# Halved inverse steps in every quarter, more adding transfers, and a shared first rounding copy, in a kernel of an FNet layer beside an S4D convolution

## The chip, the cores and the metric

One core of a Trainium2 chip. Times are device microseconds of one launch; the kernel before took 569.42 us (median of three runs, 568.53 to 570.57). TensorE's granted clock was 0.998 of full speed.

## The reference

Two independent layers over 2048 positions and 512 channels of float32, laid side by side in the output:

```python
def _A_ref(x, dft_seq_re, dft_seq_im, dft_hid_re, dft_hid_im):
    a = jnp.einsum("bsd,ed->bse", x, dft_hid_re)
    b = jnp.einsum("bsd,ed->bse", x, dft_hid_im)
    return jnp.einsum("ts,bse->bte", dft_seq_re, a) - jnp.einsum("ts,bse->bte", dft_seq_im, b)

def _B_ref(u, log_A_real, A_imag, C_real, C_imag, log_dt, D_skip):
    dt = jnp.exp(log_dt)
    A = -jnp.exp(log_A_real) + 1j * A_imag
    C = (C_real + 1j * C_imag) * dt[:, None]
    P = jnp.exp((A * dt[:, None])[:, :, None] * pos[None, None, :])
    K = 2.0 * jnp.einsum("dn,dnl->dl", C, P).real
    y = irfft(rfft(u_t, 2L) * rfft(K, 2L))[:, :, :L]
    return y.transpose(0, 2, 1) + u * D_skip
```

## The kernel before

**Two streams on one TensorE.** FNet (class Fnet) is dense matmul work: x is multiplied by the sequence matrices S (8 groups of 16 tiles, "s" groups) and the results, parked in DRAM as `p`, by the hidden matrices (4 groups of 8 tiles, "p" groups). For precision each float32 tile is split into a rounded part hi and a remainder lo, and each product is three matmuls (hh, lh, hl) of 128x128 by 128x512: 1920 matmuls (L312), issued three at a time in 640 steps. The SSM (class Ssm) builds exponential tables on VectorE, forms the kernel K by small matmuls (L735), and convolves by two-stage Fourier transforms with small tiled matmuls (L779, L840, L975, L1009, L1133, L1098), interleaved with FNet's steps.

**How a moving tile is split.** A plain tile is loaded by SP into `raw` (L266), rounded into hi by ScalarE (L150) and subtracted into lo by VectorE (L155): `split`. A soft tile, one of `SOFTS`, is loaded by GpSimd's queue straight into hi with the rounding done by the transfer (L248); ScalarE writes -hi into lo (L251), and a second GpSimd transfer adds the source to lo (L253). There are five hi/lo pairs (DEPTH) and five raw buffers (RAWS). SOFTS holds 5 of the 16 tiles of each of the groups 1 to 7, 35 in all. The first S tile is loaded by ScalarE's queue, and TensorE's first product waits for it.

**The inverse steps.** Channels go in four quarters h of 128. After the second-stage products, `first_inverses` (L1009) writes a partial inverse through `zs` in DRAM; the last stage loads it again as `zl`. Quarters 0 and 1 use `inverse`: 16 matmuls with 128 rows of contraction and 64 columns for each of two blocks (L1133; the profile counts each float32 matmul twice, so x32). Quarters 2 and 3 (HALVED) use `inverse2`: VectorE first forms sum and difference of the two halves (L1089, L1091), then 32 matmuls (x64) with half the rows and 32 columns, eight side by side in the array (L1098). Quarter 2's two blocks run as one pair, quarter 3's as (3,0) and (3,1). Both kinds write 512 KB of output (L1145, L1119). Their constants are `ib`, and `ib2`, which is loaded over ib's place once the four old blocks are done (`load_ib2`).

**The order** of all instructions is written out by hand: `ORDER` lists, entry by entry, which generator goes one step further, and `TURNS` who takes PSUM banks next. Each engine and queue runs its share in that order. FNet's matmul generator is number 31 in the old list (640 entries of three matmuls) and 30 in the new. In the old tail 491 is product (3,3) with its first inverse (its fifth entry), 477 the pair of quarter 2, 494 and 505 the blocks (3,0) and (3,1); in the new one these are 496, 481, 497 and 505. An inverse's entries are its four load issues, its VectorE passes, its matmul block and its evictions. y tiles d0 to d3 of the last FNet group are evicted by ScalarE (L326, L321) and stored (L335, L322).

Of the kernel before, what the change touches and what calls it, by code (L numbers as in the profile page):

```python
# [26 lines left out]
def fft_constants():  # L27
# [24 lines left out]
    return [np.ascontiguousarray(a.astype(np.float32)) for a in (f1u, f1k, w2, ia, ib, ib2)]  # L52
# [70 lines left out]
class Fnet:  # L123
# [23 lines left out]
    def split(self, *tiles, n=None):  # L147
        yield "act"
        hi, _, src = tiles if n is None or n > 1 else self.first[self.turns["hi"].pop(0)]
        self.nc.scalar.activation(hi, src, AF.Copy)  # L150
        if not self.hi_ev.done:
            self.plan.set(self.hi_ev)
        yield "dve"
        hi, lo, src = tiles if n is None or n > 1 else self.first[self.turns["lo"].pop(0)]
        self.nc.vector.tensor_tensor(lo, src, hi.bitcast(F32), op=OP.subtract)  # L155
# [102 lines left out]
    def load(self, src, to, where, key, ev):  # L258
# [11 lines left out]
        yield from self.split(*to, raw)  # L270
# [76 lines left out]
class Ssm:  # L347


    def __init__(self, tc, ctx, plan, fnet, nd, ldt, dsk, uG, f1u, f1k, w2, ia, ib, ib2, out):  # L350
        self.tc, self.nc, self.plan, self.fnet = tc, tc.nc, plan, fnet
        self.nd, self.ldt, self.uG, self.ib2_in, self.out = nd, ldt, uG, ib2, out
# [8 lines left out]
        second, third = (("w2", w2), ("ib", ib)), (("ia", ia),)  # L361
# [8 lines left out]
        self.sets, self.set_ev, self.ib_ev, self.ib_left = {}, [Event(), Event()], Event(), 4  # L370
# [501 lines left out]
    def quarters(self):  # L872
# [11 lines left out]
        self.ib2_ev, self.loaded_ev = Event(), Event()  # L884
        self.pair, self.last, self.k_ev = [[] for _ in range(4)], [], Event()
        self.plan.spawn(self.load_ib2())
# [51 lines left out]
    def product(self, b, h, q, got, done):  # L938
# [65 lines left out]
        def run(got, o=0):  # L1004
            for c in range(2):
                for g in range(2):
                    for xx in range(4):
                        rows = slice(32 * xx, 32 * xx + 32)
                        nc.tensor.matmul(got[xx // 2][1][64 * g:64 * g + 64, xx % 2, o:o + 2 * PART], self.ia[rows, q // 2 if h >= HALVED else 0, c],  # L1009
                                         Y[c][rows, :, g], start=c == 0, stop=c == 1, tile_position=(32 * xx, 64 * g))  # L1010
# [42 lines left out]
    def inverses(self, h):  # L1053

        yield self.zs_ev[h][0]
        if h < 3:
            yield self.zs_ev[h][1]
        if h >= HALVED:
            yield self.set_ev[1]
        b = self.sets[int(h >= min(HALVED, 3))]  # L1060
        for i in range(2):
            yield b.zls
            self.plan.spawn((self.inverse2 if h >= HALVED else self.inverse)(b, h, i, 16))

    def load_ib2(self):
        yield self.ib_ev
        self.ib2 = self.ib[:, :16].rearrange("p n (a s) -> p n a s", a=2)
        yield "dma"
        self.nc.sync.dma_start(self.ib2, self.ib2_in)
        self.plan.set(self.ib2_ev)  # L1070

    def inverse2(self, b, h, i, n):
# [6 lines left out]
        for a in range(2):  # L1079
            yield self.zs_ev[h][a]  # L1080
            yield "act"
            nc.scalar.dma_start(z[64:, a], view[:, a, n * i + c:n * i + n])
            yield "dma"
            nc.sync.dma_start(z[:64, a], view[:, a, n * i:n * i + c])
        t = b.pool.tile([128, c, PART], F32, name="zsum", bufs=2 * b.n - 1)
        for w in range(0, c, 4):
            m = slice(w, w + 4)
            yield "dve"
            nc.vector.tensor_tensor(t[:, m], z[:, 0, m], z[:, 1, m], op=OP.add)  # L1089
            yield "dve"  # L1090
            nc.vector.tensor_tensor(z[:, 1, m], z[:, 0, m], z[:, 1, m], op=OP.subtract)  # L1091
# [13 lines left out]
        yield self.ib2_ev  # L1105
        got = yield from self.banks(len(two))
        yield "pe"
        for (_, _, run), (_, ps) in zip(two, got):
            run(ps)
        for (i, z, _), (k, ps) in zip(two, got):  # L1110
# [11 lines left out]
    def inverse(self, b, h, i, n):  # L1122

        nc = self.nc
        z = b.pool.tile([128, n, PART], F32, name="zl", bufs=b.n)
        yield "dma"
        for o in range(0, n, 8):
            nc.sync.dma_start(z[:, o:o + 8], self.zs[h].rearrange("s c l d -> (s c) l d")[:, n * i + o:n * i + o + 8])
        (k, ps), = yield from self.banks(1)
        yield "pe"  # L1130
        for w in range(n // 2):
            for y in range(2):
                nc.tensor.matmul(ps[64 * y:64 * y + 64, w // 4, PART * (w % 4):PART * (w % 4) + PART],  # L1133
                                 self.ib[:, n * i + 2 * w + y], z[:, 2 * w + y], start=True, stop=True,
                                 tile_position=(0, 64 * y))
        self.ib_left -= 1
        if not self.ib_left:
            self.plan.set(self.ib_ev)
        o = n * i // 2
        for w in range(0, n // 2, 4):  # L1140
            yield "act"
            nc.scalar.activation(z[:, w:w + 4], ps[:, w // 4].rearrange("p (w d) -> p w d", w=4), AF.Copy)
        self.give(k)
        yield "dma"
        nc.sync.dma_start(self.out[:, o:o + n // 2, PART * h:PART * h + PART], z[:, :n // 2])  # L1145
        self.plan.put(b.zls)


ORDER = [
# [185 lines left out]
```

## Time and profile before

| what | value |
|---|---|
| three runs, median | 569.42 us |
| profiled execution | 569.5 us, its span 567.7 us |
| TensorE busy | 559.3 us (99%), 6278 matmuls |
| VectorE busy | 505.6 us (89%) |
| ScalarE busy | 369.5 us (65%) |
| GpSimd busy | 50.3 us (9%) |
| DMA | 135.5 MB, 239 GB/s mean |
| chain that ended last, by line | L312 79%, L735 5%, L975 5%, L1009 3%, L840 2%, L779 1%, L1133 1%, L1098 1% |

How to read it: the span runs from the first to the last instruction of the profiled execution; the 1.8 us between it and the execution's time lie around it. PE is TensorE's matmuls, DVE VectorE, ACT ScalarE, POOL GpSimd, SP the queue that issues most DMAs; a q after an engine's name is its sequencer or DMA issue. "Lnnn" is a line of the kernel. The chain follows back, from the last instruction, what released each step. A wait's "issue" means that nothing the profile shows was waited for.

### The profile page before, as it was taken

How to read it: one execution, taken by the hardware profiler on the slowest of the kernel's cores; microseconds unless marked ns; L12 is line 12 of the kernel's file. 1: busy time of each engine (PE TensorE's matmuls, PEld its weight loads, DVE VectorE, ACT ScalarE, POOL GpSimd, SP SyncE). 2: the span in 40 equal slices, each digit the busy share in tenths (PEclk: the TensorE clock that was granted, in tenths of full speed). 3: DMA queues.
4: the chain of work that ended last, by engine and by line, in shares of the span. 5: the costliest groups of instructions: out<-in, count | busy, mean ns of one | idle time of the engine just before them, and what ended most of it. 6: DMA issues, size and time to landing. Idle time of an engine off the chain costs nothing.

```text
span 567.7 us, 15512 instructions
## 1 busy us (share of the span) xinstructions
PE 559.3 (99%) x6278; PEld 433.0 (76%) x6278; DVE 505.6 (89%) x846; ACT 369.5 (65%) x734; POOL 50.3 (9%) x74
## 2 busy tenths in 40 slices
PE   8999999999999999999999999999999999999995
PEld 6877776777878777777778778778787777777784
DVE  6979999999999999999999999999999998366640
ACT  5788736756686586868677776867876554355512
POOL 0001210021121112011111111111110000000000
PEclk9999999999999999999999999999999999999999
DMA  8989989998869858978799599679997899989776
GB/s 287 310 277 362 243 250 255 316 242 221 188 179 221 233 137 229 254 160 216 208 266 257 150 241 255 177 197 230 287 275 208 266 261 294 265 257 244 210 218 204
DMA packets 148855, 135.53 MB, mean 239 GB/s; under 512 B 47280, under 2 KB 107312, under 8 KB 148528
## 3 DMA queue, kind: packets, MB, share of 16 engines
q1 hardware_dynamic: 137776, 113.70, 67.2%
q0 software_dynamic: 10080, 18.35, 16.3%
q10 hardware_dynamic: 928, 2.49, 1.7%
q8 instruction: 49, 0.80, 0.6%
q14 instruction: 22, 0.18, 0.1%
HBM read 91.79 MB, written 42.73 MB: 237 GB/s over the span
## 4 chain that ended last, share of the span: by engine, by line
PE 98%; DMA 1%; ACT 0%; issue 0%
PE acc L312 79%; PE f L735 5%; PE f L975 5%; PE f L1009 3%; PE f L840 2%; PE f L779 1%; PE f L1133 1%; PE f L1098 1%; DMA raw<-in_sT 1%; ACT hi L150 0%; ACT y L321 0%; ACT zl L1113 0%
## 5 line engine op out<-in xcount | busy, mean ns | idle before, releaser
L312 PE MATMUL acc<-hi,x 128*128 128x512 f32 x1280 | 344.0, 395 | 0.3 <-ACT hi L150 0.3
L312 PEld LDWEIGHTS acc<-hi,x 128*128 128x128 f32 x1280 | 236.3, 188 | 67.5 <-issue 16.3
L312 PE MATMUL acc<-lo,x 128*128 128x512 f32 x640 | 189.6, 391 | 0.3 <-issue 0.3
L312 PEld LDWEIGHTS acc<-lo,x 128*128 128x128 f32 x640 | 119.7, 188 | 28.8 <-issue 3.3
L150 ACT ACTIVATE hi<-raw 128x512 fp32r<-128x512 f32 x125 | 77.2, 627 | 39.8 <-PE acc L312 19.3
L155 DVE TENSOR_TENSOR lo<-raw,hi 128x512 fp32r<-128x512 f32 x125 | 84.7, 686 | 20.0 <-ACT hi L150 15.6
L531 DVE TENSOR_TENSOR prod<-t,cs 128x128 f32<-128x128 f32 (+4 forms) x128 | 87.2, 695 | 1.1 <-ACT t L678 0.5
L547 ACT ACTIVATE square<-t 128x256 f32<-128x256 f32 (+1 forms) x64 | 36.8, 576 | 30.1 <-DVE t L540 25.8
L540 DVE TENSOR_TENSOR t<-prod 128x64 f32<-128x64 f32 (+4 forms) x128 | 53.0, 426 | 0.9
L253 POOL DMA_DIRECT2D lo<-in_sT x35 | 30.5, 872 | 246.6 <-ACT lo L251 134.0
L642 DVE TENSOR_TENSOR t<-t,cs 128x1024 f32<-128x1024 f32 x32 | 39.0, 1222 | 0.3
L648 DVE TENSOR_TENSOR t<-t,prod 128x1024 f32<-128x1024 f32 x32 | 39.1, 1221 | 0.1
L642 DVE TENSOR_TENSOR prod<-t,cs 128x1024 f32<-128x1024 f32 x32 | 39.0, 1220 | 0.0
L947 ACT ACTIVATE uk<-f 128x1024 f32<-128x1024 f32 x32 | 31.3, 1020 | 10.2 <-PE f L975 10.1
L326 ACT ACTIVATE y<-acc 128x512 f32<-128x512 f32 x47 | 26.7, 597 | 13.0 <-PE acc L312 13.0
L735 PEld LDWEIGHTS f<-t,t 128*32 128x32 f32 x2048 | 29.3, 110 | 5.5 <-issue 4.1
L248 POOL DMA_DIRECT2D hi<-in_sT x35 | 21.9, 626 | 127.2 <-PE acc L312 105.9
L735 PE MATMUL f<-t,t 128*32 128x64 f32 x2048 | 31.9, 220 | 0.0
L1037 ACT ACTIVATE z<-f 128x512 f32<-128x512 f32 x32 | 17.5, 603 | 19.8 <-PE f L1009 12.4
L251 ACT ACTIVATE lo<-hi 128x512 fp32r<-128x512 f32 x35 | 21.8, 624 | 10.6 <-DMA hi<-in_sT 10.3
L962 DVE TENSOR_TENSOR z<-uk 128x1024 f32<-128x1024 f32 (+1 forms) x20 | 20.1, 1009 | 7.4 <-ACT uk L947 7.3
L560 DVE TENSOR_TENSOR t<-square 128x128 f32<-128x128 f32 (+1 forms) x64 | 24.8, 388 | 1.1 <-ACT square L547 1.1
(107 smaller groups left out, 509.0 us busy)
## 6 DMA issues: line engine op xcount, KB each, us to landing
raw<-in_sT SPq DMA_DIRECT2D x92, 256.0 KB, 5.2
hi<-in_sT POOLq DMA_DIRECT2D x35, 256.0 KB, 5.7
lo<-in_sT POOLq DMA_DIRECT2D x35, 256.0 KB, 5.7
p<-y SPq DMA_DIRECT2D x32, 256.0 KB, 4.8
xk<-xk_sb SPq DMA_DIRECT2D x32, 256.0 KB, 4.7
zs<-z SPq DMA_DIRECT2D x32, 256.0 KB, 3.6
raw<-p SPq DMA_DIRECT2D x32, 256.0 KB, 5.1
xt<-xu SPq DMA_DIRECT2D x24, 256.0 KB, 5.1
```

The lines of the kernel that those rows point to most:

```text
L150: self.nc.scalar.activation(hi, src, AF.Copy)
L155: self.nc.vector.tensor_tensor(lo, src, hi.bitcast(F32), op=OP.subtract)
L253: self.nc.gpsimd.dma_start(lo, src, accum_op=OP.add)
L312: self.nc.tensor.matmul(acc[d], still["hl".index(p[0])][:, 128 * d:128 * d + 128], m["hl".index(p[1])], start=i is items[0] and p == "hh", ...
L531: self.nc.vector.tensor_tensor(p.rearrange("p k d c m -> p k (d c) m"), src.rearrange("p d c l -> p (d c) l")[:, None, :, rows].to_broadca ...
L540: self.nc.vector.tensor_tensor(dst[:, :, :, rows], p[:, 0], p[:, 1, :, ::-1], op=OP.add)
L547: self.nc.scalar.activation(sq, t[:, :, :, m // 2:m], AF.Square)
L642: self.nc.vector.tensor_tensor(dst, t[:, :, :, rows], seed[:, k, :, :, None].to_broadcast([128, CHUNK, 2, n // 2 // CHUNK]), op=OP.mult)
L648: self.nc.vector.tensor_tensor(dst, dst, p[:, :, ::-1], op=OP.add)
L735: nc.tensor.matmul(ps[32 * j:32 * j + 32, i], t1[:, d, c], t2[:, d, c], start=c == 0, stop=c == 1, tile_position=(0, 32 * j))
L947: a.activation(uk[:, r].rearrange("p g c n d -> p g (c n d)"), p, AF.Copy)
L975: nc.tensor.matmul(got[r][1][32 * xx:32 * xx + 32, g, 256 * c:256 * c + 256], self.w2[rows, 2 * q + r, xx, 32 * c:32 * c + 32], xt[rows].r ...
```

## The change

`inverse` and `load_ib2` go; the old `inverse2`, renamed `inverse`, serves all four quarters, with whole instead of halved VectorE passes, and for quarters 0 and 1 with its sum in a buffer of the z pool, which has three buffers in the first set instead of two. Only `ib2` is kept as a constant, and the output is unpacked on the host in one form. SOFTS holds 8 of 16 tiles of each group instead of 5, 56 in all. `split` takes a column `half`: for the first S tile ScalarE rounds columns 0 to 255 and VectorE columns 256 to 511. ORDER and TURNS are new throughout. The hunks that only rename or drop `ib` and the greater part of the order are left out.

```diff
-    def split(self, *tiles, n=None):
+    def split(self, *tiles, n=None, half=None):
         yield "act"
         hi, _, src = tiles if n is None or n > 1 else self.first[self.turns["hi"].pop(0)]
-        self.nc.scalar.activation(hi, src, AF.Copy)
+        self.nc.scalar.activation(hi[:, :half], src[:, :half], AF.Copy)
+        if half:
+            self.nc.vector.tensor_copy(hi[:, half:], src[:, half:])
...
-        yield from self.split(*to, raw)
+        yield from self.split(*to, raw, half=256 if key == self.items[self.groups[0]][0] else None)
...
-        second, third = (("w2", w2), ("ib", ib)), (("ia", ia),)
+        second, third = (("w2", w2), ("ib2", ib2)), (("ia", ia),)
...
-        self.plan.spawn(self.load_ib2())
...
-                        nc.tensor.matmul(got[xx // 2][1][64 * g:64 * g + 64, xx % 2, o:o + 2 * PART], self.ia[rows, q // 2 if h >= HALVED else 0, c],
+                        nc.tensor.matmul(got[xx // 2][1][64 * g:64 * g + 64, xx % 2, o:o + 2 * PART], self.ia[rows, q // 2, c],
...
-        yield self.zs_ev[h][0]
-        if h < 3:
-            yield self.zs_ev[h][1]
-        if h >= HALVED:
+        for a in range(1 + (h < 3)):
+            yield self.zs_ev[h][a]
+        if h > 1:
             yield self.set_ev[1]
-        b = self.sets[int(h >= min(HALVED, 3))]
+        b = self.sets[int(h > 1)]
         for i in range(2):
             yield b.zls
-            self.plan.spawn((self.inverse2 if h >= HALVED else self.inverse)(b, h, i, 16))
-
-    def load_ib2(self):
-        yield self.ib_ev
-        self.ib2 = self.ib[:, :16].rearrange("p n (a s) -> p n a s", a=2)
-        yield "dma"
-        self.nc.sync.dma_start(self.ib2, self.ib2_in)
-        self.plan.set(self.ib2_ev)
-
-    def inverse2(self, b, h, i, n):
+            self.plan.spawn(self.inverse(b, h, i, 16))
+
+    def inverse(self, b, h, i, n):
 
         nc, c = self.nc, n // 2
         z = b.pool.tile([128, 2, c, PART], F32, name="zl", bufs=2 * b.n - 1)
         view = self.zs[h].rearrange("(a s) c l d -> (s c) a l d", a=2)
         if h == 2:
             yield self.loaded_ev
-        for a in range(2):
-            yield self.zs_ev[h][a]
-            yield "act"
-            nc.scalar.dma_start(z[64:, a], view[:, a, n * i + c:n * i + n])
+        if h < 2:
             yield "dma"
-            nc.sync.dma_start(z[:64, a], view[:, a, n * i:n * i + c])
-        t = b.pool.tile([128, c, PART], F32, name="zsum", bufs=2 * b.n - 1)
-        for w in range(0, c, 4):
-            m = slice(w, w + 4)
-            yield "dve"
-            nc.vector.tensor_tensor(t[:, m], z[:, 0, m], z[:, 1, m], op=OP.add)
-            yield "dve"
-            nc.vector.tensor_tensor(z[:, 1, m], z[:, 0, m], z[:, 1, m], op=OP.subtract)
+            for y in range(2):
+                nc.sync.dma_start(z[64 * y:64 * y + 64], view[:, :, n * i + c * y:n * i + c * y + c])
+            yield b.zbs
+            t = b.pool.tile([128, c, PART], F32, name="z", bufs=b.zn)
+        else:
+            for a in range(2):
+                yield self.zs_ev[h][a]
+                yield "act"
+                nc.scalar.dma_start(z[64:, a], view[:, a, n * i + c:n * i + n])
+                yield "dma"
+                nc.sync.dma_start(z[:64, a], view[:, a, n * i:n * i + c])
+            t = b.pool.tile([128, c, PART], F32, name="zsum", bufs=2 * b.n - 1)
+        yield "dve"
+        nc.vector.tensor_tensor(t, z[:, 0], z[:, 1], op=OP.add)
+        yield "dve"
+        nc.vector.tensor_tensor(z[:, 1], z[:, 0], z[:, 1], op=OP.subtract)
...
-        yield self.ib2_ev
         got = yield from self.banks(len(two))
         yield "pe"
         for (_, _, run), (_, ps) in zip(two, got):
             run(ps)
+        if h < 2:
+            self.plan.put(b.zbs)
         for (i, z, _), (k, ps) in zip(two, got):
             for y in range(2):
...
-    def inverse(self, b, h, i, n):
...
 ORDER = [
...
-    485, 31, 485, 481, 31, 493, 492, 486, 31, 492, 31, 493, 31, 493, 468, 31, 491, 482, 31, 491, 31, 483, 478, 31,
-    477, 471, 31, 477, 489, 491, 494, 477, 494, 481, 478, 31, 478, 491, 487, 31, 495, 478, 491, 477, 31, 496, 491, 31,
-    491, 498, 31, 483, 497, 477, 499, 500, 482, 489, 482, 31, 477, 489, 31, 477, 483, 502, 31, 504, 487, 31, 477, 487,
-    31, 31, 501, 496, 31, 494, 496, 31, 494, 31, 31, 31, 505, 31, 505, 501, 31, 31, 31, 497, 31, 503, 494, 31, 494,
-    502, 31, 494, 495, 31, 494, 31, 501, 505, 31, 505, 31, 503, 494, 503, 31, 494, 31, 494, 477, 31, 506, 31, 31, 505,
-    31, 499, 505, 31, 507, 31, 505, 31, 505, 31, 510, 505, 508, 509, 31, 505, 505, 511, 512,
...
+    490, 493, 30, 494, 30, 480, 30, 492, 30, 494, 496, 480, 498, 470, 496, 481, 499, 475, 30, 500, 481, 479, 30, 486,
+    30, 499, 487, 481, 500, 497, 499, 488, 500, 489, 491, 30, 481, 496, 495, 30, 481, 491, 481, 30, 496, 503, 481, 30,
+    502, 496, 501, 504, 502, 486, 497, 488, 486, 30, 496, 30, 496, 496, 30, 508, 487, 30, 496, 30, 489, 505, 30, 509,
+    489, 30, 30, 495, 505, 30, 495, 30, 487, 30, 488, 501, 30, 498, 30, 507, 30, 497, 30, 497, 30, 505, 30, 30, 505,
+    30, 30, 507, 506, 30, 507, 30, 30, 497, 504, 30, 30, 497, 30, 505, 30, 497, 505, 30, 497, 497, 505, 510, 512, 30,
+    505, 30, 505, 513, 30, 514, 511, 515,
 ]
...
 CHUNK, FIRST = 32, 128
-HALVED = 2
-ZS = 2, 4
+ZS = 3, 4
 RAWS, DEPTH, STAGED = 5, 5, 4
-SOFTS = {(g, k) for g in range(1, 8) for k in (2, 5, 8, 11, 14)}
+SOFTS = {(g, k) for g in range(1, 8) for k in range(1, 16, 2)}
 BATCH = 2
```

## Rows read from the trace of the kernel before

**Rows 1.** The profile page, busy time of TensorE: us, share of the span, instructions.

```profile
PE 559.3 (99%) x6278; PEld 433.0 (76%) x6278; DVE 505.6 (89%) x846; ACT 369.5 (65%) x734; POOL 50.3 (9%) x74
```

**Rows 2.** The chain that ended last, in order of time: start us, us, what.

```profile
166.71 21.31 PE acc L312 x93
...
280.46 1.90 PE f L1133 x32
...
529.08 1.91 PE f L1009 x64
...
551.79 1.09 PE f L1098 x64
552.88 7.04 PE acc L312 x30
559.92 1.12 PE f L1098 x64
```

**Rows 3.** Waits of TensorE, whole run: us in total, times, longest.

```profile
PE f L1133 <- issue: 0.4, 1, 0.4
...
PE acc L312 <- issue: 0.3, 1, 0.3
```

**Rows 4.** Windows of 50 us, VectorE: us, busy us (instructions), granted clock, DMA share, GB/s.

```profile
50.00:100.00 50.00, 48.17 (x80) 1.00 0.93 263
100.00:150.00 50.00, 49.38 (x85) 1.00 0.90 253
...
400.00:450.00 50.00, 48.84 (x82) 1.00 0.90 260
450.00:500.00 50.00, 39.31 (x62) 1.00 0.95 265
```

**Rows 5.** Lines L248 and L253, the hi transfer, then the adding one: issue to landing.

```profile
DMA to landing us min/median/max: 3.0/5.7/9.1
...
DMA to landing us min/median/max: 3.9/5.7/8.2
```

**Rows 6.** Timeline of the start: start us, us, engine, line, operation, tiles, shapes, count.

```profile
4.15 0.63 ACT L150 ACTIVATE hi<-raw 128x512 fp32r<-128x512 f32 x1 [1.68 <-DMA raw<-in_sT]
4.16 0.29 DVE L195 TENSOR_TENSOR x<-uk,x 128x128 fp32r<-128x128 f32 x1
...
4.81 0.69 DVE L155 TENSOR_TENSOR lo<-raw,hi 128x512 fp32r<-128x512 f32 x1 [0.35 <-ACT hi L150]
...
5.55 0.50 PE L312 MATMUL acc<-lo,x 128*128 128x512 f32 x1
```

**Rows 7.** Timeline of the end, VectorE, ScalarE and the SP queue in turn.

```profile
544.79 0.69 DVE L1089 TENSOR_TENSOR zsum<-zl 128x512 f32<-128x512 f32 x1 [3.34 <-DMA zl<-zs]
...
551.70 0.69 DVE L1089 TENSOR_TENSOR zsum<-zl 128x512 f32<-128x512 f32 x1 [2.04 <-DMA zl<-zs]
...
561.06 1.09 ACT L1113 ACTIVATE zl<-f 128x512 f32<-128x512 f32 x2 [0.21 <-PE f L1098]
...
563.05 0.43 SPq L1119 DMA_DIRECT2D out_yb<-zl  x1
```

**Rows 8.** Groups by form, VectorE and ScalarE: count, busy us, mean ns of one.

```profile
L962 DVE TENSOR_TENSOR z<-uk 128x1024 f32<-128x1024 f32 x12 | 14.7, 1222 | 0.0
...
L193 DVE CAST x<-uk 128x128 fp32r<-128x128 f32 x1 | 0.2, 227 | 2.4 <-DMA uk<-in_x 2.4
...
L576 ACT ACTIVATE seed<-seed 128x256 f32<-128x256 f32 x16 | 6.7, 419 | 0.5
```

**Rows 9.** Waits, all engines: us in total, times, longest.

```profile
ACT lo L251 <- DMA hi<-in_sT: 10.3, 4, 5.3
```

**Rows 10.** DMA queues from 50 to 440 us: packets, MB, share of 16 engines.

```profile
q1 hardware_dynamic: 88930, 70.15, 61.0%
q0 software_dynamic: 9936, 18.09, 23.5%
```

**Rows 11.** DMA issues by line, whole run: count, size, median us to landing.

```profile
out_ya<-y SPq DMA_DIRECT2D x15, 256.0 KB, 5.4
```

More of the change, by code (lines that the diff above doesn't have):

```diff
@@ L51, in fft_constants @@
     ib2 = ib[:64].reshape(64, 2, 2, 8, 32, 2).transpose(2, 0, 1, 3, 5, 4).reshape(128, 16, 2, 32)
-    return [np.ascontiguousarray(a.astype(np.float32)) for a in (f1u, f1k, w2, ia, ib, ib2)]
+    return [np.ascontiguousarray(a.astype(np.float32)) for a in (f1u, f1k, w2, ia, ib2)]
 class Sem:
@@ L347, with __init__ @@
 class Ssm:
-    def __init__(self, tc, ctx, plan, fnet, nd, ldt, dsk, uG, f1u, f1k, w2, ia, ib, ib2, out):
+    def __init__(self, tc, ctx, plan, fnet, nd, ldt, dsk, uG, f1u, f1k, w2, ia, ib2, out):
         self.tc, self.nc, self.plan, self.fnet = tc, tc.nc, plan, fnet
-        self.nd, self.ldt, self.uG, self.ib2_in, self.out = nd, ldt, uG, ib2, out
+        self.nd, self.ldt, self.uG, self.out = nd, ldt, uG, out
         self.const = ctx.enter_context(tc.tile_pool(name="b_const", bufs=1))
@@ L369, in __init__ @@
         self.pars = Sem(1)
-        self.sets, self.set_ev, self.ib_ev, self.ib_left = {}, [Event(), Event()], Event(), 4
+        self.sets, self.set_ev = {}, [Event(), Event()]
         self.const_ev, self.const2_ev, self.const3_ev, self.xu_ev = Event(), Event(), Event(), Event()
@@ L883, in quarters @@
         self.plan.spawn(self.products())
-        self.ib2_ev, self.loaded_ev = Event(), Event()
+        self.loaded_ev = Event()
         self.pair, self.last, self.k_ev = [[] for _ in range(4)], [], Event()
-        self.plan.spawn(self.load_ib2())
         for h in range(4):
@@ L1120, in store_y @@
         self.plan.put(b.zls)
-    def inverse(self, b, h, i, n):
[L1124 to L1146, printed above, removed]
-ORDER = [
[104 rows of a table removed]
+ORDER = [
[106 rows of a table added]
 ]
 TURNS = [
[3 rows of a table removed]
[3 rows of a table added]
 ]
 CHUNK, FIRST = 32, 128
-HALVED = 2
-ZS = 2, 4
+ZS = 3, 4
 RAWS, DEPTH, STAGED = 5, 5, 4
-SOFTS = {(g, k) for g in range(1, 8) for k in (2, 5, 8, 11, 14)}
+SOFTS = {(g, k) for g in range(1, 8) for k in range(1, 16, 2)}
 BATCH = 2
@@ L1273, in program @@
         b = Ssm(tc, ctx, plan, a, i["nd"], i["ldt"], i["dsk"], i["uG"], i["f1u"], i["f1k"], i["w2"], i["ia"],
-                i["ib"], i["ib2"], o["yb"])
+                i["ib2"], o["yb"])
         tables = Event()
@@ L1291, in layout @@
     n = lambda a: np.asarray(a)
-    f1u, f1k, w2, ia, ib, ib2 = fft_constants()
+    f1u, f1k, w2, ia, ib2 = fft_constants()
     w = np.stack([n(A_dft_hid_re).T, n(A_dft_hid_im).T])
@@ L1306, in layout @@
         uG=u.reshape(32, 2, 16, 2, DM).transpose(3, 1, 0, 2, 4).reshape(128, 16, DM),
-        f1u=f1u, f1k=f1k, w2=w2, ia=ia, ib=ib, ib2=ib2)
+        f1u=f1u, f1k=f1k, w2=w2, ia=ia, ib2=ib2)
     return {k: np.ascontiguousarray(v) for k, v in arrays.items()}
@@ L1314, in assemble @@
 def assemble(ya, yb):
-    n = PART * HALVED
-    y1 = yb[:, :, :n].reshape(2, 64, 16, n).transpose(1, 2, 0, 3).reshape(SEQ, n)
-    y2 = yb[:, :, n:].reshape(2, 2, 32, 2, 2, 4, DM - n).transpose(2, 1, 3, 4, 5, 0, 6).reshape(SEQ, DM - n)
-    return np.concatenate([ya.T, y1, y2], axis=1)[None]
+    y = yb.reshape(2, 2, 32, 2, 2, 4, DM).transpose(2, 1, 3, 4, 5, 0, 6).reshape(SEQ, DM)
+    return np.concatenate([ya.T, y], axis=1)[None]
 def kernel(**inputs):
```

204 rows, old and new, of tables (ORDER, TURNS) are left out of this document.

## Prediction

> **What bounds the kernel now.** First the page's busy times: TensorE works 559.3 of 567.7 us [rows 1]. A busy TensorE need not be a fast one, so next the chain of work that ended last, in order of time: from the first FNet matmul to the last it is TensorE blocks end to end, and in between the whole list has two gaps, 0.4 and 0.3 us [rows 2, 3]. So a TensorE microsecond removed is a microsecond gained, provided that nothing else comes late, and any other engine's microsecond is worth nothing by itself. Two views tell how close "late" is: the table by windows, where VectorE is busy up to 49.4 of 50 us and the DMA engines 0.90 to 0.95 of the time in the four fullest [rows 4], and the landing times of the adding transfers [rows 5]. The two ends of the run, before TensorE starts and after it stops, are read in the timeline [rows 6, 7].
>
> The chain also prices a boundary. A stretch of 30 FNet matmuls takes 7.04 us and one of 93 takes 21.31 [rows 2]: (21.31 - 7.04)/63 = 0.2265 us a matmul and 0.245 us for each stretch, that is, for each change from FNet to SSM work and back.
>
> **Halved steps.** An old inverse block of quarters 0 and 1 is 1.90 us of TensorE; the halved kind, already used for quarters 2 and 3, is 1.09 and 1.12 us [rows 2]. Four blocks change kind: 4 x (1.90 - 1.10) = **-3.2 us**, on the path, with the boundaries unchanged. If two of them came as a pair the gain would be nearer 3.7. One old block had a 0.4 us gap inside [rows 3]; it may go with the block or be found elsewhere: 0 to -0.4, I take **-0.2**, the middle, since no row tells its cause. What the halving adds is two VectorE passes of 128x1024 for each block, 1.22 us each [rows 8]: 8 x 1.22 = 9.8 us. TensorE now waits for them, and they stand in VectorE's queue among the table work; the block also takes a z buffer, of which there are three instead of two. They are hidden if VectorE is not overloaded, which the next part pays for: 21 subtractions of 0.69 us [rows 6] leave, 14.5 us. Net VectorE -4.7 us while TensorE shortens by 3.2: the little idle time it has [rows 4] stays. ScalarE's two evictions for each block stay too. The old constant (1 MB, then overwritten by 0.5 MB) becomes one load of 0.5 MB; TensorE's waits [rows 3] name no load of it.
>
> **More adding transfers.** 56 soft S tiles instead of 35. Each of the 21 replaces one SP load, one ScalarE rounding and one VectorE subtraction by two POOL transfers with a ScalarE negation between them. ScalarE's work is the same; SP issues 21 fewer. The negation waits for the first transfer at the head of ScalarE's queue, with the other tiles' roundings behind it, a wait that cost 10.3 us in four cases before [rows 9], off the path. The DMA engines pay. Between 50 and 440 us the software queue held 23.5% of 16 engines for 18.09 MB, that is 1466 engine-us for 69 transfers of 0.262 MB, 21.2 each; the hardware queue held 61.0% for 70.15 MB, 14.2 for the same size [rows 10]. So 42 x 21.2 - 21 x 14.2 = 592 engine-us more, 9.5% of that stretch. Where the share was 0.93 and 0.90 [rows 4] it would become 1.02 and 1.00.
>
> Does that reach TensorE? FNet takes 160 moving tiles in 557 us, one in 3.48, so five hi/lo pairs are 17.4 us of lead. A soft tile needs 5.7 us for the first transfer, 0.63 for a pass of ScalarE [rows 6], 5.7 for the second: 12.0 at the medians, 17.9 with both at their longest [rows 5]. Before, no wait of TensorE ended with such a transfer; its two gaps after the start, 0.7 us together, came with 35 soft tiles [rows 3]. Scaled by 56/35 they become 1.1: I take **+0.4**. Ends: -0.3 (the second gap gone) and +7.8 (below). The row it is nearest to is that of the gaps, because the medians leave 5 us.
>
> The Trainium skill would make this nothing at all: "DMA: Bandwidth & Descriptors", section "Anatomy of one DMA — SWDGE (gpsimd) path", gives such a transfer 2.0 us plus its bytes over 436 GB/s, an estimate of 2.6 us for 256 KB, and by it the term would be 0 and the sum 565.3. The trace disagrees: the median is 5.7 us [rows 5], and the engines are 0.93 busy at 263 GB/s [rows 4]. I go by the rows.
>
> **The first S tile.** Before: ScalarE rounds it from 4.15 to 4.78, VectorE subtracts from 4.81 for 0.69, and the third matmul of the start, which needs lo, goes at 5.55 [rows 6]. ScalarE's half should take about 0.42 (a 128x256 pass, [rows 8]), so the first matmul starts some 0.2 us earlier. But VectorE's copy stands ahead of its 0.29 us subtraction for x, and that ahead of lo. The copy is 128x256; a 128x128 cast takes 0.23 [rows 8], so 0.23 to 0.36. From 4.15: 0.36 + 0.29 + 0.69 and two gaps of 0.02 give lo at 5.53; with 0.23, 5.40. Before it was 5.50. The third matmul gains between -0.03 and +0.1, and what the first two gained is waited away there. I take **-0.05**.
>
> **New order.** I cannot time 2,700 entries one by one. The number of SSM blocks is the same, 67, and 65 stretches lie between; if two more blocks are parted it costs 0.5, if four more meet it saves 1.0 (0.245 each). I take 0.
>
> **New end.** The order's tail can be read. Before, product (3,3)'s last block stands 38 FNet steps before the end, then the paired block of quarter 2, then (3,0) with 11 steps left and (3,1) with one. After: the pair with 35 left, (3,3)'s block with 31, (3,0) with 4, (3,1) with 3. Two consequences.
>
> One: after the last inverse there are 9 matmuls instead of 3, so its eviction and 512 KB store run beside TensorE. Take the end of that block as 0. Before: TensorE ended at 0.92 (3 x 0.2265 + 0.245), ScalarE's two evictions took 1.09, the y tile's came next (a 128x512 pass, 0.63 [rows 6]), SP issued the store behind the y tile's at 563.05, and the run ended 4.65 us later [rows 7], at 567.7 - 561.04 = 6.66, that is 5.74 after TensorE. After: TensorE ends at 2.28; evictions done at 1.1, d2's y tile at 1.75, the store issued at about 2.2 and 4.65 more: 6.85, that is 4.57 after TensorE. The gain is 1.17 if the store lands as before. But three y tiles and (3,0)'s 512 KB now fly beside it, and d1's y tile is issued at 2.65 behind it: with 5.4 us, the median of such stores before [rows 11], it would end at 8.05 and gain nothing. Nearer to the row is the first (the same store, at the end of the run): **-0.8**, ends 0 and -1.2.
>
> Two: the reload. (3,0) and (3,1) need (3,3)'s results stored, loaded again and added. Before, VectorE got (3,0)'s data at 544.79, 13.8 us after the block of (3,3) ended, (3,1)'s at 551.70, 20.7 after [rows 7]. Now 27 steps of 0.68 and a boundary, 18.6 us, lie before (3,0) and 20.6 before (3,1). The first needs 13.8 + 2.44 = 16.2: in time. The second at the old pace needs 23.1: 2.5 late. But its buffer was one that the pair's output had to leave, and the pair now stands four steps ahead of (3,3) instead of seven behind, 7.5 us sooner. I take 0, ends 0 and +2.5.
>
> **Sum** against the profiled execution (567.7 us span, 569.5 us in all, the median of three being 569.42): -3.2 - 0.2 + 0.4 - 0.05 - 0.8 = -3.85, so **565.7 us**, span 563.9.
>
> **Rivals.** (A) Crowding, half hidden: the share stops at 0.95, the highest of the windows [rows 4]. What exceeds it is delayed: 0.075 x 50 from 50 to 100, 0.045 x 50 to 150 and 0.045 x 40 from 400 to 440, 3.8 + 2.2 + 1.8 = 7.8 us. If the tiles' lead eats half, the time is 565.7 + 3.9 = 569.6. For: the shares. Against: the planned lead of 5 us at the medians. The Trainium skill has a rule against it: "SBUF — State Buffer", section "SBUF: two separate sides", puts the peak of the DMA ports at about 436 GB/s, by which 263 GB/s would be far from full and this rival void; the busy shares beside it speak for the rival. (B) The same, exposed, ends slower: once hi's issue to lo's landing passes 17.4 us, every soft tile in groups 1, 2 and 7 holds TensorE, and the whole 7.8 comes out: 573.5. For: the longest landings already make 17.9. Against: both longest at once were seen in no tile that stopped TensorE. (C) The reload is late at the end by the 2.5 worked out above: 568.2. (D) The halving saves nothing in place, since the blocks wait on VectorE for what they gain: 568.9.
>
> **Chances.** Forecast 0.62, A 0.17, B 0.13, C 0.06, D 0.02. What this kernel's measurement can tell from no change is about 0.3%, 1.7 us: faster means under 567.7. The forecast lies there with its own range, 563.3 (all terms at their good ends, two blocks met) to 567.7; A, C and D lie within: faster 0.62, same 0.25, slower 0.13. The range leaves out B and the last corner of the good ends: 563.6 to 570.3.
>
> **What would show it.** The chain of the changed kernel should have four more blocks of 1.1 us of the halved kind and no 1.90; gaps of TensorE should stay near 1 us in sum. A wait of TensorE that ends with a POOL transfer, in 50 to 150 or 400 to 440, shows A or B; one that ends with VectorE's sums before a halved block shows D or, at the end, C. The third matmul should start within 0.1 us of 5.55. From TensorE's last matmul to the end of the span should be 4.6 to 5.7 us. What would make it wrong above all: landings of adding transfers with a median of 8 us or more.

## The result, and the profile after

The changed kernel took 578.5 us (median of six, 574.8 to 580.9) beside 569.9 for the kernel before (six, 568.5 to 572.3): a ratio of 1.0147, with an interval of 1.0105 to 1.0188. It is slower; 565.7 was forecast, and the range ended at 570.3. The profiled execution took 579.3 us with a span of 577.5, 9.8 us more than before.

The page's busy line (engine, us, share of the span, instructions) and its list of DMA queues (packets, MB, share of 16 engines), changed kernel:

```profile
PE 562.0 (97%) x6406; PEld 433.6 (75%) x6406; DVE 503.7 (87%) x826; ACT 369.1 (64%) x734; POOL 80.3 (14%) x116
...
q1 hardware_dynamic: 134608, 107.15, 64.1%
q0 software_dynamic: 16128, 29.37, 25.6%
...
q8 instruction: 50, 0.82, 0.6%
```

Before, TensorE was busy 559.3 of 567.7 us [rows 1]; now it is 562.0 of 577.5. The stops are in the list of TensorE's waits, which held 0.7 us after the start [rows 3]. Changed kernel: us in total, times, longest (left out is one at the very start, which both kernels have):

```profile
PE f L781 <- issue: 3.4, 1, 3.4
PE f L737 <- issue: 2.1, 2, 1.8
...
PE acc L314 <- ACT y L328: 0.6, 1, 0.6
PE f L1096 <- DVE zl L1089: 0.5, 1, 0.5
PE f L1096 <- issue: 0.5, 1, 0.5
```

With one more of 0.3 us behind VectorE's t (L650) that is 7.4 us, 6.0 of it "issue": TensorE waited for nothing that the profile shows. No line names a POOL transfer, and in the median the adding transfers land no later than before, though the longest are 1.2 and 1.6 us longer [rows 5]. Lines L250 (hi) and L255 (lo), issue to landing:

```profile
DMA to landing us min/median/max: 2.9/5.6/10.3
...
DMA to landing us min/median/max: 4.0/5.5/9.8
```

The chain of the changed kernel (start us, us, what), first an undisturbed block of line 781 with the FNet stretch behind it, then the longest stop:

```profile
117.23 1.05 PE f L781 x32
118.28 13.83 PE acc L314 x60
...
371.86 1.03 PE f L781 x26
372.88 3.43 issue
376.32 1.12 PE f L781 x6
377.44 17.18 PE acc L314 x63
394.62 1.09 PE f L1096 x64
```

Three stretches around the stop (us, TensorE's busy time, granted clock, DMA share, GB/s):

```profile
364.00:370.00 6.00, 6.00 (x147) 1.00 1.06 250
370.00:376.30 6.30, 2.88 (x35) 1.00 1.01 207
376.30:383.10 6.80, 6.78 (x20) 0.50 0.60 127
```

TensorE stops inside a block, after 26 of its 32 matmuls, while the DMA engines are full. Behind the stop the granted clock is at its lower level, 0.50 (1.2 GHz instead of 2.4), for 6.8 us. The 63 FNet matmuls behind it take 17.18 us; by the undisturbed 13.83 for 60, three more at 0.2265 [rows 2] would make it 14.51. That is 2.7 us, and the block's 32 matmuls take 1.03 and 1.12 us for 1.05, another 1.1. So the 3.4 us stop costs 3.8 more afterwards.

The end, ScalarE and the SP queue in turn:

```profile
570.70 0.47 SPq L1118 DMA_DIRECT2D out_yb<-zl  x1
...
570.96 0.60 ACT L323 ACTIVATE y<-acc 128x512 f32<-128x512 f32 x1 [0.18 <-PE acc L314]
...
571.59 0.36 ACTq L325 DMA_DIRECT2D out_ya<-y  x1
572.25 1.13 SPq L324 DMA_DIRECT2D out_ya<-y  x1
```

TensorE stops at 570.94, 6.56 before the end; it was 5.74 [rows 7].

**The difference as a sum.** Against +9.8: TensorE's stops +6.7 (7.4 against 0.7), what stands behind the longest, mostly at half clock, +3.8, four halved blocks at 1.09 -3.2, the end +0.8. The first stretch of FNet work ends at 37.48 instead of 37.36 although it has 138 matmuls instead of 141, which is +0.8; its matmuls take 0.63 us each up to 7.5 us, where before they take 0.39 from 5.9 on. Counted in the trace, TensorE goes back from SSM to FNet work 64 times instead of 62, at 0.245 +0.5. That makes 9.4; 0.4 us I can't place.

### The profile page after: what moved, and what is told of

The parts are those of the page before. It is cut to its first block, busy times and chain, and to the rows that moved or that the text cites. A ratio compares the mean times of both kernels' runs of the same rounds, so it can differ in the third digit from the quotient of the medians.

```text
span 577.5 us, 15773 instructions
## 1 busy us (share of the span) xinstructions
PE 562.0 (97%) x6406; PEld 433.6 (75%) x6406; DVE 503.7 (87%) x826; ACT 369.1 (64%) x734; POOL 80.3 (14%) x116
## 4 chain that ended last, share of the span: by engine, by line
PE 78%; issue 8%; DVE 8%; DMA 3%; POOL 1%; ACT 1%; DVEq 0%; POOLq 0%; ACTq 0%
PE acc L314 64%; PE f L737 4%; PE f L976 4%; DMA hi<-in_sT 2%; PE f L1010 2%; PE f L842 1%; PE f L1096 1%; DVE prod L533 1%; PE f L781 1%; DVE lo L157 1%; DMA raw<-p 1%; DVE prod L644 1%; DVE t L542 1%; DVE t L644 1%; POOL hi L250 1%
## 5 line engine op out<-in xcount | busy, mean ns | idle before, releaser
L533 DVE TENSOR_TENSOR prod<-t,cs 128x1024 f32<-128x1024 f32 (+4 forms) x128 | 87.9, 695 | 4.4 <-ACT t L659 2.8
L157 DVE TENSOR_TENSOR lo<-raw,hi 128x512 fp32r<-128x512 f32 x104 | 70.6, 685 | 23.5 <-ACT hi L150 17.5
L150 ACT ACTIVATE hi<-raw 128x512 fp32r<-128x512 f32 (+1 forms) x104 | 64.0, 623 | 30.8 <-DMA raw<-p 14.7
L255 POOL DMA_DIRECT2D lo<-in_sT x56 | 49.2, 879 | 184.3 <-ACT lo L253 121.8
L250 POOL DMA_DIRECT2D hi<-in_sT x56 | 33.9, 617 | 173.1 <-PE acc L314 138.0
L253 ACT ACTIVATE lo<-hi 128x512 fp32r<-128x512 f32 x56 | 34.9, 623 | 29.3 <-DMA hi<-in_sT 19.2
L650 DVE TENSOR_TENSOR t<-t,prod 128x1024 f32<-128x1024 f32 x32 | 39.0, 1219 | 0.1
L328 ACT ACTIVATE y<-acc 128x512 f32<-128x512 f32 x47 | 27.3, 596 | 13.0 <-PE acc L314 13.0
L976 PE MATMUL f<-xt,w 64*32 64x256 f32 x768 | 23.5, 379 | 0.0
```

What stands on the lines that cost most here:

```text
L150: self.nc.scalar.activation(hi[:, :half], src[:, :half], AF.Copy)
L250: self.nc.gpsimd.dma_start(hi, src)
L255: self.nc.gpsimd.dma_start(lo, src, accum_op=OP.add)
L533: self.nc.vector.tensor_tensor(p.rearrange("p k d c m -> p k (d c) m"), src.rearrange("p d c l -> p (d c) l")[:, None, :, rows].to_broadca ...
L650: self.nc.vector.tensor_tensor(dst, dst, p[:, :, ::-1], op=OP.add)
L976: nc.tensor.matmul(got[r][1][32 * xx:32 * xx + 32, g, 256 * c:256 * c + 256], self.w2[rows, 2 * q + r, xx, 32 * c:32 * c + 32], xt[rows].r ...
```

## The experiments

Where do the "issue" stops come from? One thing stands out when TensorE's instructions are counted from the start: weight loads, matmuls, and the 105 semaphore waits and drains that the trace shows in its queue (108 before). The four of the changed kernel come after 2498, 6850, 8129 and 12226 of them: 9 x 256 + 194, 26 x 256 + 194, 31 x 256 + 193, 47 x 256 + 194. (The 0.5 us put down to VectorE's zl comes after 5312, 20 x 256 + 192, and may be a fifth.) The queue "q8 instruction" brought 0.82 MB in 50 packets, 16.4 KB each, and 2 x 6406 + 105 instructions are 50.5 times 256; before it was 49 packets for 49.5 times 256. So I took it that TensorE's instructions come in pages of 256 through the same DMA engines as the data, and that it stops where a page is late. The Trainium skill has this, in "Runtime: NRT & Kernel Launch", section "Instruction fetch mechanics": 16 KiB blocks of 256 instructions on a DMA queue of the engine's own, and a crossing that is "mostly hidden". The counts agree, and so do most of the 50 crossings, which show no stop; the four stops, 3.4 us the longest, do not.

Why late here and not before? Theory 1, **places**: dense blocks (a taps block is 256 instructions in 1.9 us) fall badly across the pages in the new order. Theory 2, **crowding**: the further adding transfers fill the DMA engines, and a page waits behind them. Theory 3, forecast's rival B: the soft tiles themselves come late.

**Fewer bytes in the adding transfers.** Only 64 of 512 columns are added, for k in (3, 9, 13), 21 tiles, and then for all 56; the other columns of lo stay without their source:

```diff
-        self.nc.gpsimd.dma_start(lo, src, accum_op=OP.add)
+        m = slice(0, 64 if i[3] in (3, 9, 13) else DM)      # all 56: slice(0, 64)
+        self.nc.gpsimd.dma_start(lo[:, m], src[:, m], accum_op=OP.add)
```

> The changed kernel, but the adding transfer of the 21 further tiles brings only columns 0 to 63 of 512, so those lo tiles stay incomplete; TensorE's instructions, their order and number are the same. Theory 1 (places: TensorE's instructions arrive in pages, and dense blocks of small matmuls run out of them where a page boundary falls badly in the new order): TensorE's waits put down to 'issue', about 6.3 us in the changed kernel's profile, stay at the same lines and sum to 4 to 8, time 576 to 579. Theory 2 (crowding: the 21 further adding transfers hold up the pages): the waits fall below 2 us, the half clock after the 3.4 us gap goes with them, time 569 to 572. Theory 3 (the soft tiles themselves come late): as theory 2 in time, but the waits that go would be on the POOL queue, of which the profile shows none.

> The changed kernel with all 56 adding transfers bringing only columns 0 to 63 of 512 (their lo tiles incomplete); with 21 of them so cut it took 575.3, uncut 578.5. Crowding: the sum of TensorE's gaps falls on, from 7.4 and 4.9 us to under 2, time 569 to 572. Places alone: gaps stay 4 to 6, 575 to 577.

Measured: 575.3 us with 21 cut (572.7 to 578.4, ratio 1.0088, 1.0056 to 1.0119) and 573.3 with 56 (570.8 to 575.3, 1.0045, 1.0027 to 1.0064). Uncut it is 1.0147: the time falls with the bytes, by 5 us in all, with the order untouched. TensorE's waits with 56 cut:

```profile
PE f L782 <- issue: 2.4, 1, 2.4
...
PE acc L315 <- ACT y L329: 0.6, 1, 0.6
PE f L1097 <- issue: 0.6, 1, 0.6
PE f L738 <- issue: 0.3, 1, 0.3
```

The stops sum to 3.9 us instead of 7.4 (4.8 with 21 cut), and behind the longest the granted clock stays at 1.00 in this profile (with 21 cut it is 0.50 for half as long as in the changed kernel). Crowding is a cause, but the expectation for it was under 2 us and 572 at most: the stop in the forward block stayed, at 2.4.

**The same traffic in the old order.** Kernel before, for k in (3, 9, 13) of groups 1 to 7:

```diff
+        if extra:
+            self.nc.gpsimd.dma_start(spare[:, :DM], src)
         ...
+            self.nc.gpsimd.dma_start(spare[:, :DM], src, accum_op=OP.add)
```

> The kernel before with 42 further 256 KB transfers on the POOL queue, two at each of 21 S tiles (the second one adding), into memory that nothing reads: the traffic of the change's adding transfers without its order, halved blocks or end (and more, since the S tiles' plain loads on SP's queue stay). Theory 1 (places): 'issue' waits stay under 1.5 us, 569 to 571. Theory 2 (crowding): they grow to 3 us or more, 572 to 580.

Measured: 578.5 us (575.6 to 583.2), ratio 1.0150 (1.0086 to 1.0213): as slow as the changed kernel, with nothing changed but these transfers. Waits of TensorE:

```profile
PE acc L319 <- ACT hi L151: 1.2, 2, 1.1
PE f L982 <- issue: 1.2, 1, 1.2
PE f L982 <- DMA xt<-xk: 1.1, 2, 0.9
```

So traffic alone slows the old order as much. But not by pages: the expectation for crowding was "issue" stops of 3 us or more, and they sum to 1.4, of which only 0.2 (L1140, after 9153 instructions) stands 193 past a multiple of 256; the 1.2 above does not. Here the data came late: a loaded tile and ScalarE's hi, and 1.0 us more hung on VectorE's zl (L862). All its stops sum to 4.7 us (0.7 before) in a profiled execution whose span is 6.6 longer; what the rest is stays open. Its traffic is also heavier than the change's (the plain loads stay): 273 GB/s over the span against 241.

**Pages moved.** The warming matmuls were replaced so that all work behind them stands 60 or 120 instructions later in the pages:

```diff
-        for n in range(3):
-            self.nc.tensor.matmul(ps[:, :256], z[:, :128], z[:, 256:], start=n == 0, stop=n == 2)
+        for n in range(1):
+            self.nc.tensor.matmul(ps[:, :256], z[:, :128], z[:, 256:], start=n == 0, stop=n == 0)
+        for n in range(32):      # 17 for 60
+            j = slice(32 * (n % 4), 32 * (n % 4) + 32)
+            self.nc.tensor.matmul(ps[j, :64], z[:, :32], z[:, 256:320], start=True, stop=True, tile_position=(0, 32 * (n % 4)))
```

> The changed kernel with the 3 warming matmuls replaced by one of 256 columns and 17 small ones: TensorE's instruction stream behind them is later by 60 instructions, all work and its order unchanged. Theory 1 (places): the gaps move to other blocks; by counting which blocks then hold a boundary 193 instructions in, hardly one dense block does, so the 'issue' waits sum to under 2 us and the time is 570 to 573. Theory 2 (crowding): the sum of gaps stays 5 to 8 us, 576 to 580. Theory 3 (late data): the gaps stay at the same lines and program places, 576 to 579.

> As the run with 60 instructions more, but 120 (one matmul of 256 columns and 32 small ones). Theory 1 (places): by the count this is near the worst placing, more dense blocks holding a boundary: 'issue' waits sum to 6 to 12 us, time 577 to 585. Theory 2 (crowding): the same 5 to 8 us whichever way it is shifted, 576 to 580. Theory 3 (late data): gaps at the same program places as in the changed kernel.

> The kernel before with its TensorE instruction stream later by 120 (one warming matmul of 256 columns and 32 small ones instead of three of 256). Places alone: as many dense blocks hold a boundary as in the changed kernel shifted so, which lost 3.6 us against unshifted; gaps 4 to 9 us, 573 to 578. Crowding: pages are in time at the traffic of before wherever the boundaries fall; gaps under 2 us, 569 to 571. Both together (late page and dense block must meet): between, gaps 2 to 4 us, 571 to 573.

Measured, changed kernel: 576.4 us for 60 (ratio 1.0113, 1.0086 to 1.0140) and 582.1 for 120 (1.0191, 1.0157 to 1.0225). Waits of TensorE, 60 and then 120:

```profile
PE acc L317 <- issue: 2.7, 1, 2.7
...
PE f L979 <- issue: 0.9, 2, 0.6
PE f L740 <- issue: 0.7, 1, 0.7
```

```profile
PE f L740 <- issue: 6.2, 2, 4.1
PE acc L317 <- issue: 3.3, 2, 1.8
```

The stops went to other lines, and the counts in front of them stayed: with 60 more the stops of 2.7, 0.7 and 0.3 us come after 8129, 8897 and 10178 instructions, with 120 more the five come after 1217, 1729, 5314, 8897 and 10178, every one 193 or 194 past a multiple of 256. (One of 0.6 us, with 60 more, comes after 2813, which is not; I can't place it.) That shows the pages. It also fells theory 3, by which the same blocks would stop. Places decide how much is lost, 576 to 582 for the same work, and 120 lost most, as theory 1 had counted. But theory 1 alone is wrong too, twice: by its count 60 should have lost under 2 us and lost 4.3, the largest stop in FNet work five matmuls behind a taps block, which it had not counted; and in the kernel before the shift by 120 changed nothing: 569.5 us, ratio 0.9993 (0.9979 to 1.0007), one "issue" stop of 0.2, as crowding alone had it (both together was put at 571 to 573). **A late page and 256 instructions run through quickly ahead of it must meet.**

How late the pages are can be read from the times of the packets on q8. Let a page be entered at 193 instructions, 449 and so on, and the n-th packet belong to the n-th entry (the numbers agree: 50 and 50, 49 and 49). Then a packet starts 1.3 us after the entry in the median and 6.0 at the latest in the changed kernel, 0.9 and 4.9 in the kernel before, 0.9 and 5.4 with 56 tiles cut, and 1.5 and 4.0 with the added traffic in the old order, which hardly stopped for pages. The packet that the 3.4 us stop waited for started 5.7 us after the entry into the page before it. So single packets were nearly as late before, and even there stops occur: 0.7 us in the profile above, and 0.8 and 1.5 at such counts in that of the run with the first tile shared, below.

**One late page taken apart.** In the changed kernel 2.75 MB were issued from 360.8 to 367.1 us, 1 MB of it two loads for the third inverse block, which VectorE wanted only at 382.8. First their entry was moved 8 FNet steps later, then behind a load at which SP waits (with the block's two VectorE steps each 3 FNet steps later in the list):

```diff
 ORDER: ... 51, 341, 324, 30 ...   ->   ... 50, 30, 341, 325, 351 ...   (8 FNet steps later)
 ORDER: ... 51, 341, 324, 30 ...   ->   ... 51, 352, 341, 51, 30 ...   (11 FNet steps later)
```

> The changed kernel with one entry of the order moved: the two 512 KB loads of the third inverse block (issued at 363.8, wanted by VectorE at 382.8) stand 8 FNet steps, 5.4 us, later, behind instead of ahead of the moment (about 368) at which TensorE's page with the taps and the forward block is called for. Some 3 MB were issued from 360.8 to 367.1 before it. Theory (a page waits behind the transfers issued just ahead of it): the 3.4 us gap inside L781 falls under 1.5, the half clock after it goes, the time is 573 to 576. Rival (the gap belongs to the block or to the page, whatever is issued): it stays 2.4 to 3.4 and the time 577 to 580.

> As the run with the moved entry, which did not delay the loads (SP waited for nothing and issued them at 363.1 all the same). Here the third inverse block's two 512 KB loads stand behind the par load, at which SP waits until 376, and its two VectorE passes 4 and 3 FNet steps later, so that 1 MB less is issued in the 7 us before TensorE calls for its page at about 368. Theory (a page waits behind the transfers issued just ahead of it): the page is 2 to 4 us sooner, the 3.2 us gap inside L781 falls under 1, the half clock after it goes, and the time is 572 to 576 unless VectorE's later sums cost TensorE a wait of their own, which the profile would name. Rival (the gap belongs to the block, whatever is issued): the gap stays 2.4 to 3.4 and the time 577 to 580.

Measured: the first 578.0 us (ratio 1.0140, 1.0115 to 1.0164), the 3.2 us stop still there. It tested nothing: SP waited for nothing there, and issued the loads at 363.1 all the same. The second 575.8 (1.0127, 1.0070 to 1.0184). The interval overlaps the changed kernel's, so no gain in time is shown, and the verdict is that of one profiled execution. TensorE's timeline, and the stretches that answer to those above:

```profile
367.35 1.99 PE L737 MATMUL f<-t,t 128*32 128x64 f32 x128
...
371.54 1.12 PE L781 MATMUL f<-ks,f1k 32*64 32x256 f32 x32
372.58 0.96 PE L314 MATMUL acc<-lo,x 128*128 128x512 f32 x3
```

```profile
364.00:370.00 6.00, 6.00 (x147) 1.00 0.91 233
370.00:376.30 6.30, 6.30 (x56) 1.00 0.49 63
376.30:383.10 6.80, 6.80 (x31) 1.00 1.09 232
```

With 1 MB less in front of it the page is there: the forward block runs through, and the half clock is gone. When the page came can be read from the queue list of narrow windows. Changed kernel, none from 368 to 373.7 us, one from 373.7 to 375; here one from 369.4 to 370.6:

```profile
q1 hardware_dynamic: 388, 1.18, 97.2%
q0 software_dynamic: 58, 0.10, 10.0%
q14 instruction: 1, 0.01, 0.7%
```

```profile
q0 software_dynamic: 151, 0.28, 91.8%
...
q8 instruction: 1, 0.02, 5.4%
```

```profile
q8 instruction: 1, 0.02, 5.0%
```

The price came at once, in its list of TensorE's waits:

```profile
PE f L737 <- issue: 2.5, 2, 2.0
PE f L1096 <- DVE zl L1089: 1.9, 1, 1.9
```

VectorE's later sums held TensorE 1.9 us at the block itself, and the medians differ by 2.7 (by the ratios 0.2%, some 1.1) where the stop and what followed it had cost 7.2. Nor is the half clock gone from every execution: two of this version's five have a mean granted clock of 0.991, as low as in the changed kernel (0.991 to 0.994), the other three 0.997 or 0.998.

**Halving alone**, in the old order and with 35 adding tiles:

```diff
+        t = b.pool.tile([128, c, PART], F32, name="zsum", bufs=1)
+        yield "dve"
+        nc.vector.tensor_tensor(t, z[:, 0], z[:, 1], op=OP.add)
+        yield "dve"
+        nc.vector.tensor_tensor(z[:, 1], z[:, 0], z[:, 1], op=OP.subtract)
```

> The kernel before, with its own order and its 35 adding tiles, with only the four inverse blocks of quarters 0 and 1 halved (two VectorE passes each, queued six FNet steps ahead of their block; the halved constant loaded once). If the halving pays what the forecast said: TensorE's work 3.2 us less, time 566 to 568. Rival D (VectorE has no room without the further adding tiles: 99% busy, 9.8 us more for it): TensorE waits on VectorE's sums or on lo, together 3 us or more, and the time is 569 to 574.

Measured: 585.8 us (584.9 to 586.4), ratio 1.0269 (1.0252 to 1.0286), worse than any expectation. Waits, of TensorE and the one of VectorE for the blocks' loads:

```profile
PE f L735 <- DVE t L560: 2.4, 1, 2.4
PE f L975 <- ACT ks L741: 2.1, 1, 2.1
...
DVE zsum L1130 <- DMA zl<-zs: 8.8, 3, 4.2
```

TensorE stopped 15.6 us, mostly for results of VectorE and ScalarE that came late. VectorE had 9.4 us more to do (515.0 busy against 505.6) and stood 8.8 at the head of its queue waiting for the blocks' loads. Lack of room and my place for the passes may both have done this, and this run doesn't part them. It does say that the halving doesn't come by itself: rival D, in the old order, is worse than 568.9.

**The first tile alone, and the old end with its last two stores exchanged:**

```diff
+        self.nc.scalar.activation(hi[:, :half], src[:, :half], AF.Copy)
+        if half:
+            self.nc.vector.tensor_copy(hi[:, half:], src[:, half:])
-ORDER: ... 505, 505, 511, 512      +ORDER: ... 505, 505, 512, 511      (second run only)
```

> The kernel before with only the first S tile's rounding copy shared between ScalarE and VectorE. Forecast: first matmul 0.4 us sooner, third matmul between 0.03 later and 0.14 sooner, time 569.4 to 570.6, no difference from before. Rival (the earlier start under half clock costs the changed kernel part of its loss): 571.5 or more.

> The kernel before with the first tile shared and the last out_yb store issued ahead of the last y tile's instead of behind it: SP would issue it at 562.2 instead of 563.05, as soon as its evictions are done. If the issue sets the end: 0.8 us less, 569.4 to 569.7 beside 570.3. Rival (the stores' bytes set the end, whichever is issued first, as the changed kernel's six stores suggest): 570 to 570.6.

Measured: 569.7 us, ratio 0.9994 (0.9979 to 1.0009), and 570.0, 0.9992 (0.9974 to 1.0010). The share costs and gains nothing, and the end is not set by which store is issued first. None of the versions beat the kernel before.

## Why the prediction was wrong, step by step

- **What bounds the kernel.** Right: the loss is TensorE's, in its list of waits and in its clock.
- **Halved steps, -3.2 and -0.2.** The -3.2 is right in size: the blocks take 1.09. The 0.4 us gap behind the -0.2 was a page's and not the block's (see the next point). Their VectorE work stayed out of the way in the new order except for one 0.5 us wait (L1089); whether it would have without the further adding tiles, the halving run can't tell.
- **More adding transfers, +0.4.** This step failed. Its traffic was right: 9.5% of the engines from 50 to 440 us were forecast, and the queues hold 9.2% more there than before [rows 10]. In the first two windows of 50 us the shares are 1.00 and 0.98, for 1.02 and 1.00 forecast [rows 4]:

```profile
q1 hardware_dynamic: 83150, 62.54, 56.5%
q0 software_dynamic: 15744, 28.68, 37.2%
```

```profile
50.00:100.00 50.00, 49.40 (x81) 1.00 1.00 281
100.00:150.00 50.00, 49.55 (x86) 1.00 0.98 270
```

  What was wrong is whom it hits. I asked when lo lands and found 5 us of lead, which held. I scaled the two old stops, 0.7 to 1.1 us, without asking what those "issue" stops were: they stand 194 and 193 past a multiple of 256 as well, and so were late instruction pages already. A page has no lead of five tiles. By the packets it comes only after the page before is entered, 1.3 us in the median, and is wanted 256 TensorE instructions later, which in the dense parts is a few microseconds (1.9 for a taps block). Where the forecast had +0.4, TensorE lost 10.5 us, 6.7 of stops and 3.8 behind the longest, beyond the upper end of 7.8 that I had put beside it, and for another reason. Some 5 us go with the adding transfers' bytes, by the two cut runs; the rest stays with all 56 cut, and the moved loads point at what else the new order issues at one time.
- **New order, 0.** Failed too. It was taken from a count of blocks, which can't show that 1 MB of loads is issued just ahead of a dense stretch. The order also has two more changes of work (+0.5) and a 0.6 us wait for ScalarE's y (L328), which every profile in the new order shows but the one shifted by 120.
- **First S tile, -0.05.** Right by its own run. In the changed kernel the third matmul starts at 5.41, not 5.55 [rows 6], 0.14 sooner, slightly more than I allowed. Its timeline:

```profile
4.37 0.69 DVE L157 TENSOR_TENSOR lo<-raw,hi 128x512 fp32r<-128x512 f32 x1
...
5.41 0.63 PE L314 MATMUL acc<-lo,x 128*128 128x512 f32 x1
```

- **New end, -0.8.** Wrong in sign: 6.56 us after TensorE instead of the 4.57 to 5.77 forecast. The out_yb store was issued where I had put it and landed 4.2 us later, 3.6 before (the 4.65 of the forecast runs on to the end of the span). What I set aside, the stores that fly with it, came last: 1.58 MB moved after TensorE's last matmul, against 1.13 before, and the last half tile, issued at 572.25 behind a busy queue, landed last, at 576.5. That their bytes set the end fits this and the exchanged stores, but no run took them away. The reload (rival C) was in time: TensorE ran 81 FNet matmuls and both last blocks without a stop.
- **Rivals.** Crowding was there as A and B had it in the shares, and B's 573.5 had the sign. But its mechanism, soft tiles that hold TensorE, was seen in no run, and neither A nor B had a price for pages or for the clock.
- **The Trainium skill** on the adding transfers ("DMA: Bandwidth & Descriptors", section "Anatomy of one DMA — SWDGE (gpsimd) path") came out as the rows had it: the median is 5.5 us and not the 2.6 estimated from it. What I hadn't weighed are the instruction blocks of "Runtime: NRT & Kernel Launch" in the Trainium skill, cited above; that crossing them is "mostly hidden" did not hold for the four that stopped TensorE, 6.0 us together.

## What to carry to other kernels

Look at an "issue" stop inside a TensorE block before scaling it: count the engine's instructions up to it, its semaphore waits too, and if the count sits at one place modulo 256 in every case, suspect an instruction page, which came through the same DMA engines as the data here. In a kernel whose DMA share is near 1.0, extra bytes cost by what they make late for whoever has least lead: pages in the new order, tiles in the old one. The dearest single place here was a burst issued just ahead of a dense block of small matmuls. Where VectorE or TensorE is relieved by moving work onto the DMA engines, cost the bursts in windows of a few microseconds, not of 50.

## What the hardware showed that I had not expected

- TensorE's instructions come in 16.4 KB packets, one for 256 of them. When 2.75 MB were issued in the 6 us before one was wanted, TensorE stood for 3.4 us; with 1 MB less it did not stand there at all in the profiled execution.
- Behind that 3.4 us stop the granted clock was 0.50 for 6.8 us, most of the 3.8 us lost there. It went away with the stop. The length of a stop alone does not tell: one of 2.7 us in the run shifted by 60 (mean granted clock 0.997) and one of 2.4 with 56 tiles cut had no such stretch behind them, but in the run shifted by 120 one of 1.8 us had 3.4 us at 0.50 behind it.
